# Attention decode backward on one core: long weight rows, gradients in place, scores of 32 rows, a zero fill issued alone

## The chip, the core and the metric

The kernel runs on one core of a Trainium2 chip. Times are device microseconds of that core. The kernel before takes 797.53 us, the median of two runs (797.41 and 797.66). The profile is one execution recorded by the hardware profiler, whose span, from the first to the last instruction, is 795.6 us.

## The reference

One decode step (two batches, one token, width 512) goes through a layer norm into two branches: attention over the last 4,096 of 32,768 cached positions, and a small MLP with squared ReLU. The output is `x + s * silu(u)`. All gradients are returned too.

```python
xn = layernorm(x)
q  = xn @ wq                                  # 32 heads of 128, 4 per K/V head
k, v = k_cache[:, :, -4096:], v_cache[:, :, -4096:]
p  = softmax(q @ k^T * 128**-0.5)
s  = (p @ v) @ wo
u  = relu(xn @ w1 + b1)**2 @ w2 + b2
out = x + s * silu(u)
# outputs: out, and d/d(x, k_cache, v_cache, wq, wo, w1, b1, w2, b2) for grad_out
```

The gradients of the two caches have the shape of the caches (2 x 8 x 32,768 x 128, 134 MB each). Outside the window of 4,096 positions they are zero, and the kernel has to write those zeros: 32 regions of 28,672 rows of 256 bytes, 234.88 MB.

## The kernel before

**Queues.** GpSimd (POOL) issues the zero fill, SyncE (SP) the loads of K, V, `w1`, `w2` and the last stores, ScalarE (ACT) the loads of `wq` and `wo` and the stores of gradients. All of them end on the same 16 DMA engines.

**Zero fill (lines 77 to 161).** The source is `zt`, 7,168 bytes of zeros per partition, which the DMA widens to bf16, so that one packet writes 14,336 bytes (56 rows of a cache). A fill covers 128 partitions x 4 such packets, a region. Every fourth region uses 32 rows a packet (8,192 bytes). `skip_plan` gives six regions a fill of 120 partitions in place of 128, which leaves one DMA engine out, after a tiny fill (`zf_tiny`) that is meant to set which. Nine fills are issued first (`ZF_FIRST`), the rest two or so per block between POOL's own work.

**Prologue (lines 205 to 311).** Norm, the MLP forward, and transposed copies of `w1` and `w2`.

**Blocks.** The loop over 8 K/V heads loads `wq` (two heads at once, 2,048-byte rows) and `wo` (4,096-byte rows) per head, transposes `wo`, computes q and the gradient `do` of the head's output for both batches, and has POOL build `bdq` and `bddo`: a row of q or do, repeated for 128 rows and masked by `maskbd`, 128 x 4,096, eight products of 128 x 1,024 per block (line 443). Then, for each batch (16 blocks in all): 32 transposes of K; scores as 32 products of 128 columns with a shifted window of `zq`, so that row `i * 32 + c` holds query i against chunk c; softmax over 128 x 128; 32 transposes of V; `o`; dp in the same form; `ds`; dq; and 8 + 8 outer products (lines 531 and 538) that make dv and dk in `dv_st` and `dk_st`, one buffer each. The gradient of `wo` for a head (`o_dependent_tail`, line 335) is made in the middle of a block and shares the `dv_st` buffer. The gradient of `wq` is stored for two heads at a time.

**Epilogue (lines 571 to 672).** The output, the MLP's backward with its two weight gradients, the gradient of x.

A scheduler orders the instructions of each engine from these dependences. The loads of block n + 1 wait until the buffers of block n - 1 (two per tensor) are free.

Of the kernel before, what the change touches and what calls it, by code (L numbers as in the profile page):

```python
# [8 lines left out]
ACT = mybir.ActivationFunctionType  # L9
# [8 lines left out]
def kernel(  # L18
# [28 lines left out]
    HQ = A_wq.shape[1] // DH  # L47
# [5 lines left out]
    DK = D // P  # L53
    SCALE = float(DH) ** -0.5
    EPS = 1e-5
    assert B == 2 and REP == 4 and NC_ == 32 and DH == P

    dma_zero = nc.gpsimd
    dma_load = nc.sync
    dma_store = nc.scalar  # L60

    const = ctx.enter_context(tc.tile_pool(name="const", bufs=1))
    attn = ExitStack()
    kvp = attn.enter_context(tc.tile_pool(name="kvp", bufs=2))
    kvt = attn.enter_context(tc.tile_pool(name="kvt", bufs=2))
    kt1 = attn.enter_context(tc.tile_pool(name="kt1", bufs=1))
    rowp = attn.enter_context(tc.tile_pool(name="rowp", bufs=1))
    wsl = attn.enter_context(tc.tile_pool(name="wsl", bufs=2))
    wsl1 = attn.enter_context(tc.tile_pool(name="wsl1", bufs=1))
    small = attn.enter_context(tc.tile_pool(name="small", bufs=3))  # L70
    hkp = attn.enter_context(tc.tile_pool(name="hkp", bufs=2))
# [4 lines left out]

    ZR = SK - W
    ZG = 56
    ZE = ZG * DH
    zt = const.tile([P, ZE], mybir.dt.uint8, name="zt")  # L80
    nc.vector.memset(zt[:].bitcast(F32), 0.0)

    zcur = [0]

    def _kof(n):
        for k in range(16, 0, -1):
            if n % k == 0:
                return k
        return 1

    def zf(o, q, r0, nent, rows_per_ent, zg=None):
        zg = zg or ZG
        b, hk = divmod(q, HKV)
        nr = nent * rows_per_ent
        if rows_per_ent % zg == 0:
            v = o[b, hk, r0:r0 + nr, :].rearrange("(r p g) d -> p r (g d)", p=nent, g=zg)
            src = zt[0:nent, 0:zg * DH].unsqueeze(1).to_broadcast([nent, rows_per_ent // zg, zg * DH])
        else:
            v = o[b, hk, r0:r0 + nr, :].rearrange("(p g) d -> p (g d)", p=nent)
            src = zt[0:nent, 0:rows_per_ent * DH]  # L100
        dma_zero.dma_start(out=v, in_=src)  # L101
        zcur[0] = (zcur[0] + _kof(nent)) % 16
        return r0 + nr

    SCRAP_Q = 2 * B * HKV - 1
    scrap_pos = [0]

    def zf_tiny(n):
        b, hk = divmod(SCRAP_Q % (B * HKV), HKV)
        p0 = scrap_pos[0]  # L110
        assert 0 < n and p0 + n <= DH
        dma_zero.dma_start(out=out_3[b, hk, ZR - 1:ZR, p0:p0 + n], in_=zt[0:1, 0:n])
        scrap_pos[0] = p0 + n
        zcur[0] = (zcur[0] + _kof(n)) % 16

    skip_plan = {3: (0, 4), 8: (4, 4), 13: (0, 4), 18: (4, 2), 23: (0, 4), 27: (3, 1)}
    ZG_OF = lambda qi: (ZG if qi % 4 != 3 else 32)
    zf_jobs = []

    def region_jobs(qi):  # L120
        o = out_2 if qi < B * HKV else out_3
        q = qi % (B * HKV)
        st = {"r": 0}

        zg = ZG_OF(qi)

        def j_skip():
            eng, nch = skip_plan[qi]
            adv = (eng + 1 - zcur[0]) % 16
            if adv:  # L130
                zf_tiny(adv)
            st["r"] = zf(o, q, st["r"], 120, nch * ZG)

        def j_main():
            rem = ZR - st["r"] - (P if qi == SCRAP_Q else 0)
            n_full = rem // (P * zg)
            if n_full:
                st["r"] = zf(o, q, st["r"], P, n_full * zg, zg)
            rem = ZR - st["r"] - (P if qi == SCRAP_Q else 0)
            if rem:  # L140
                nent = [n for n in (128, 64, 32, 16) if rem % n == 0][0]
                st["r"] = zf(o, q, st["r"], nent, rem // nent)
            if qi == SCRAP_Q:
                st["r"] = zf(o, q, st["r"], P - 1, 1)
                if scrap_pos[0] < DH:
                    zf_tiny(DH - scrap_pos[0])

        return ([j_skip] if qi in skip_plan else []) + [j_main]

    for qi in range(2 * B * HKV):  # L150
        zf_jobs.extend(region_jobs(qi))
    ZF_FIRST = 9

    def zf_issue(n):
        for _ in range(n):
            if zf_jobs:
                zf_jobs.pop(0)()

    zf_issue(ZF_FIRST)

# [3 lines left out]
    make_identity(nc, ident_f[:])  # L164
    eps_t = const.tile([P, 1], F32, name="eps_t")
    nc.vector.memset(eps_t[:], EPS)

# [16 lines left out]
    ds_rows = const.tile([B, D], BF16, name="ds_rows")  # L184

# [20 lines left out]

    with tc.tile_pool(name="pw", bufs=1) as pw:
# [6 lines left out]
        b2_bf = pw.tile([DK, P], BF16, name="b2_bf")  # L214
        dma_store.dma_start(out=b2_bf[:], in_=B_b2.rearrange("(k p) -> k p", p=P))
        w1 = pw.tile([P, DK, F], BF16, name="w1")
        dma_load.dma_start(out=w1[:], in_=B_w1.rearrange("(k p) f -> p k f", p=P))
        w2 = pw.tile([P, FK, D], BF16, name="w2")
        dma_load.dma_start(out=w2[:], in_=B_w2.rearrange("(p j) d -> p j d", j=FK))

        tp = ps_m.tile([P, DK, B], BF16, tag="m")
        for k in range(DK):
            nc.tensor.transpose(tp[:, k, :], x_bf[:, k * P:(k + 1) * P], ident_bf[0:B, 0:B])
        nc.vector.tensor_copy(out=xT_f[:], in_=tp[:])
        tp = ps_m.tile([P, DK, B], BF16, tag="m")
        for k in range(DK):
            nc.tensor.transpose(tp[:, k, :], go_bf[:, k * P:(k + 1) * P], ident_bf[0:B, 0:B])
# [4 lines left out]
        tp = ps_m.tile([P, DK], BF16, tag="m")  # L232
        nc.tensor.transpose(tp[:, :], b2_bf[:, :], ident_bf[0:DK, 0:DK])
        nc.vector.tensor_copy(out=b2T[:], in_=tp[:])
# [14 lines left out]
        tp = ps_m.tile([B, DK, P], BF16, tag="m")  # L249
        for k in range(DK):  # L250
            nc.tensor.transpose(tp[:, k, :], xnT[:, k, :], ident_bf[:, :])
        nc.vector.tensor_copy(out=xn_bf[:], in_=tp[:].rearrange("b k p -> b (k p)"))
# [12 lines left out]
        for dk in range(DK):  # L265
            for fk in range(FK):
                nc.tensor.matmul(ups[:, dk, :], lhsT=w2[:, fk, dk * P:(dk + 1) * P], rhs=h2T_bf[:, fk, :],
                                 start=(fk == 0), stop=(fk == FK - 1))
# [18 lines left out]
        tp = ps_m.tile([B, DK, P], BF16, tag="m")  # L287
        for k in range(DK):
            nc.tensor.transpose(tp[:, k, :], dsT_bf[:, k, :], ident_bf[:, :])
        nc.vector.tensor_copy(out=ds_rows[:], in_=tp[:].rearrange("b k p -> b (k p)"))  # L290
# [5 lines left out]
        for dk in range(DK):  # L296
            for fk in range(FK):
                jobs.append((w2[:, fk, dk * P:(dk + 1) * P], w2T, dk, fk * P))
# [14 lines left out]
    stage = attn.enter_context(tc.tile_pool(name="stage", bufs=1))  # L313
    bdp = attn.enter_context(tc.tile_pool(name="bdp", bufs=2))

    acc_s = const.tile([P, DK, B], F32, name="acc_s")
    nc.vector.memset(acc_s[:], 0.0)
    acc_dxn = const.tile([P, DK, B], F32, name="acc_dxn")
    nc.vector.memset(acc_dxn[:], 0.0)

    maskf = const.tile([P, NC_], F32, name="maskf")
    nc.vector.tensor_reduce(out=maskf[:], in_=ident_bf[:, :].rearrange("p (i c) -> p c i", i=REP), axis=AX.X, op=ALU.add)
    maskbd = const.tile([P, NC_, DH], BF16, name="maskbd")
    nc.vector.tensor_copy(out=maskbd[:], in_=maskf[:].unsqueeze(2).to_broadcast([P, NC_, DH]))
    NZ = 4
    zq_bufs, zdo_bufs = [], []
    for j in range(NZ):
        t = const.tile([P, 160], BF16, name=f"zq{j}")
        nc.vector.memset(t[:], 0.0)
        zq_bufs.append(t)  # L330
        t = const.tile([P, 160], BF16, name=f"zdo{j}")
        nc.vector.memset(t[:], 0.0)
        zdo_bufs.append(t)

    def o_dependent_tail(hk, oT_bf, wo_alt):
        tp = ps_m.tile([B, REP, P], BF16, tag="m")
        for i in range(REP):
            nc.tensor.transpose(tp[:, i, :], oT_bf[:, i, :], ident_bf[:, :])
        o_rows_alt = rowp.tile([B, REP, P], BF16, tag="o_rows_alt")
        nc.vector.tensor_copy(out=o_rows_alt[:], in_=tp[:].rearrange("b i d -> b (i d)").rearrange("b (p j) -> b j p", j=REP))  # L340
        tp = ps_m.tile([P, REP, B], BF16, tag="m")
        for j in range(REP):
            nc.tensor.transpose(tp[:, j, :], o_rows_alt[:, j, :], ident_bf[0:B, 0:B])
        oT_alt = hkp.tile([P, REP, B], BF16, tag="oT_alt")
        nc.vector.tensor_copy(out=oT_alt[:], in_=tp[:])
        sps = ps_m.tile([P, DK, B], F32, tag="m")
        for dk in range(DK):
            for j in range(REP):
                nc.tensor.matmul(sps[:, dk, :], lhsT=wo_alt[:, j, dk * P:(dk + 1) * P], rhs=oT_alt[:, j, :],
                                 start=(j == 0), stop=(j == REP - 1))  # L350
# [352 lines left out]
```

## Time and profile before

| what | value |
|---|---|
| median of the runs | 797.53 us |
| span of the profiled execution | 795.6 us |
| mean clock granted to TensorE | 0.691 |
| DMA, HBM read and written | 45.62 MB and 280.50 MB |
| mean us from issue to landing: K load, V load, dv store, dk store, zero fill of a region | 20.9, 16.6, 22.0, 17.1, 135.2 |
| POOL products (line 443) | 128, 267 us busy |

The profile cuts the span into 40 slices and gives the busy share of each engine and of the DMA in each. A queue's share is the time of its packets over the time of 16 engines. q0 is the zero fill, q1 what SP issues, q10 what ACT issues, q8 and q14 are instruction fetches. The waits name an idle engine, its line, and what ended its idle time.

### The profile page before, as it was taken

How to read it: one execution, taken by the hardware profiler on the slowest of the kernel's cores; microseconds unless marked ns; L12 is line 12 of the kernel's file. 1: busy time of each engine (PE TensorE's matmuls, PEld its weight loads, DVE VectorE, ACT ScalarE, POOL GpSimd, SP SyncE). 2: the span in 40 equal slices, each digit the busy share in tenths (PEclk: the TensorE clock that was granted, in tenths of full speed). 3: DMA queues.
4: the chain of work that ended last, by engine and by line, in shares of the span. 5: the costliest groups of instructions: out<-in, count | busy, mean ns of one | idle time of the engine just before them, and what ended most of it. 6: DMA issues, size and time to landing. Idle time of an engine off the chain costs nothing.

```text
span 795.6 us, 11174 instructions
## 1 busy us (share of the span) xinstructions
PE 402.2 (51%) x4776; PEld 277.0 (35%) x4776; DVE 265.6 (33%) x550; ACT 210.0 (26%) x384; POOL 315.3 (40%) x249
## 2 busy tenths in 40 slices
PE   4566444573446546634475358446733686276000
PEld 3466124352424444423272326243522353131000
DVE  3243322361323423611352136223611453754000
ACT  2232310360133314501342135203600450034000
POOL 3001791098109531881080719800826192700000
PEclk9978655895588659955697589656955795555555
DMA  9999999999999999999999999999999999999981
GB/s 361 421 422 424 427 427 423 431 416 417 423 428 424 417 420 428 421 421 421 428 420 422 424 426 423 425 422 430 422 420 422 430 425 420 431 429 425 416 340 57
DMA packets 37794, 326.85 MB, mean 411 GB/s; under 512 B 3008, under 2 KB 3144, under 8 KB 11016
## 3 DMA queue, kind: packets, MB, share of 16 engines
q0 software_dynamic: 20288, 234.89, 71.6%
q10 hardware_dynamic: 11296, 50.34, 16.5%
q1 hardware_dynamic: 6160, 40.91, 13.2%
q8 instruction: 37, 0.61, 0.3%
q14 instruction: 13, 0.11, 0.0%
HBM read 45.62 MB, written 280.50 MB: 410 GB/s over the span
## 4 chain that ended last, share of the span: by engine, by line
DMA 48%; PE 19%; DVE 9%; issue 6%; ACT 5%; POOL 2%; another core or an unknown queue 2%; ACTq 0%; POOLq 0%; DVEq 0%
DMA out_dram<-dv_st 20%; DMA knat<-in_A_k_cache_dram 15%; DMA out_dram<-dwo_st 7%; DMA out_dram<-zt 5%; ACT dv_st L193 3%; DMA out_dram<-dk_st 2%; PE ov L531 2%; PE s_ps L467 2%; PE ok L538 2%; PE tp L463 2%; PE dp_ps L506 2%; PE tp L495 1%; PE dq_ps L524 1%; DVE dk_st L195 1%
## 5 line engine op out<-in xcount | busy, mean ns | idle before, releaser
L443 POOL TENSOR_TENSOR bddo<-dorep,maskbd 128x1024 bf16<-128x1024 bf16 x64 | 133.6, 2114 | 90.5 <-ACT dorep L438 90.5
L443 POOL TENSOR_TENSOR bdq<-qrep,maskbd 128x1024 bf16<-128x1024 bf16 x64 | 133.4, 2110 | 0.0
L101 POOL DMA_DIRECT2D out_dram<-zt x42 | 32.2, 769 | 203.5 <-DMA out_dram<-zt 201.8
L463 PE MATMUL tp<-ident_bf,knat 128*128 128x128 bf16 x512 | 56.6, 280 | 74.8 <-DMA knat<-in_A_k_cache_dram 71.3
L463 PEld LDWEIGHTS <-knat 128*128 128x128 bf16 x512 | 44.7, 127 | 98.8 <-DMA knat<-in_A_k_cache_dram 72.8
L193 ACT CAST dv_st<-ov 128x512 bf16<-128x512 f32 x80 | 44.4, 593 | 125.3 <-PE ov L531 81.2
L531 PE MATMUL ov<-bddo,p_blk 128*128 128x512 bf16 x128 | 51.4, 486 | 50.3 <-ACT dv_st L193 39.6
L195 DVE CAST dv_st<-ov 128x512 bf16<-128x512 f32 x48 | 33.2, 693 | 100.7 <-PE ov L531 57.9
L355 PE MATMUL wps<-ds_rows,o_rows_alt 2*128 2x512 bf16 x32 | 17.4, 600 | 73.0 <-ACT dwo_st L193 73.0
L538 PE MATMUL ok<-bdq,ds_blk 128*128 128x512 bf16 x128 | 46.2, 422 | 15.9 <-DVE dk_st L195 6.0
L195 DVE COPY kT<-tp 128x1024 bf16<-128x1024 bf16 x48 | 32.8, 682 | 58.4 <-PE tp L463 58.4
L193 ACT CAST dk_st<-ok 128x512 bf16<-128x512 f32 x80 | 44.6, 589 | 26.7 <-PE ok L538 22.5
L495 PE MATMUL tp<-ident_bf,vnat 128*128 128x128 bf16 x512 | 42.9, 235 | 7.6 <-DVE vT L195 4.5
L495 PEld LDWEIGHTS <-vnat 128*128 128x128 bf16 x512 | 36.6, 107 | 26.3 <-issue 24.4
L195 DVE CAST dk_st<-ok 128x512 bf16<-128x512 f32 x48 | 32.8, 689 | 28.1 <-PE ok L538 24.8
L195 DVE CAST dwo_st<-wps 128x512 bf16<-128x512 f32 x16 | 11.1, 691 | 85.5 <-DMA out_dram<-dv_st 81.8
L193 ACT CAST dwo_st<-wps 128x512 bf16<-128x512 f32 x16 | 8.7, 588 | 112.0 <-DMA out_dram<-dv_st 111.6
L195 DVE COPY vT<-tp 128x1024 bf16<-128x1024 bf16 x48 | 32.3, 682 | 14.7 <-PE tp L495 14.5
L531 PEld LDWEIGHTS <-p_blk 128*128 128x128 bf16 x128 | 12.7, 119 | 59.6 <-ACT dv_st L193 25.5
L538 PEld LDWEIGHTS <-ds_blk 128*128 128x128 bf16 x128 | 10.3, 103 | 40.2 <-DVE dv_st L195 17.3
L519 PEld LDWEIGHTS <-ds_blk 128*128 128x128 bf16 x16 | 1.7, 104 | 64.2 <-issue 64.2
L195 DVE COPY woT_s<-tp 128x1024 bf16<-128x1024 bf16 x8 | 19.5, 2432 | 10.5 <-PE tp L394 10.5
(240 smaller groups left out, 674.9 us busy)
## 6 DMA issues: line engine op xcount, KB each, us to landing
out_dram<-zt POOLq DMA_DIRECT2D x25, 7168.0 KB, 135.2
out_dram<-zt POOLq DMA_DIRECT2D x4, 6720.0 KB, 146.6
vnat<-in_A_v_cache_dram SPq DMA_DIRECT2D x16, 1024.0 KB, 16.6
knat<-in_A_k_cache_dram SPq DMA_DIRECT2D x16, 1024.0 KB, 20.9
out_dram<-dv_st ACTq DMA_DIRECT2D x16, 1024.0 KB, 22.0
out_dram<-dk_st ACTq DMA_DIRECT2D x16, 1024.0 KB, 17.1
out_dram<-zt POOLq DMA_DIRECT2D x1, 6144.0 KB, 100.5
out_dram<-zt POOLq DMA_DIRECT2D x1, 5120.0 KB, 98.6
```

The costliest lines, as they stand in the source:

```text
L101: dma_zero.dma_start(out=v, in_=src)
L193: nc.scalar.copy(out=out_ap, in_=in_ap)
L195: nc.vector.tensor_copy(out=out_ap, in_=in_ap)
L355: nc.tensor.matmul(wps[:], lhsT=o_rows_alt[:, j, :], rhs=ds_rows[:, :], start=True, stop=True)
L443: nc.gpsimd.tensor_tensor(out=bd[:, c0:c0 + BDC, :], in0=rep[:, :].unsqueeze(1).to_broadcast([P, BDC, DH]), in1=maskbd[:, c0:c0 + BDC, :], ...
L463: nc.tensor.transpose(tp[:, j, :], knat[:, g * 8 + j, :], ident_bf[:, :])
L467: nc.tensor.matmul(s_ps[:], lhsT=zq[:, 31 - c:159 - c], rhs=kT[:, c, :], start=(c == 0), stop=(c == NC_ - 1))
L495: nc.tensor.transpose(tp[:, j, :], vnat[:, g * 8 + j, :], ident_bf[:, :])
L506: nc.tensor.matmul(dp_ps[:], lhsT=zdo[:, 31 - c:159 - c], rhs=vT[:, c, :], start=(c == 0), stop=(c == NC_ - 1))
L524: nc.tensor.matmul(dq_ps[:], lhsT=knat[:, c, :], rhs=dsT[:, c, :], start=(c == 0), stop=(c == NC_ - 1))
L531: nc.tensor.matmul(ov[:], lhsT=p_blk[:, :], rhs=bddo[:, g * 4:(g + 1) * 4, :].rearrange("p c d -> p (c d)"), start=True, stop=True)
L538: nc.tensor.matmul(ok[:], lhsT=ds_blk[:, :], rhs=bdq[:, g * 4:(g + 1) * 4, :].rearrange("p c d -> p (c d)"), start=True, stop=True)
```

## The change

Work is moved between queues and stages; what is computed stays.

- **Weights.** `wq` and `wo` are loaded whole on SP in the prologue and stay in memory. Partition p holds four adjacent rows of `wq` (32 KB) and 32 adjacent rows of `wo` (32 KB); `w1` is laid out in the same way (14 KB), as `w2` was. q and do of all heads are computed in the prologue.
- **Gradients in place.** The gradient of `wq` is written over `wq` head by head and stored once after the loop. The gradient of `wo` is written over `wo` at the end of the epilogue and stored once. The gradients of `w1` and `w2` are made after that of x.
- **Scores.** 32 rows of 512: 8 products of 512 columns in place of 32 of 128. The softmax joins 8 groups of rows with `group_sum`, a masked 32 x 32 transpose and reduction.
- **Block diagonals.** 32 x 1,024 in place of 128 x 4,096, made by DVE from PSUM. The outer products have 32 rows to contract in place of 128.
- **Zero fill.** All 42 fills are issued one after the other, all of 128 partitions but the last pieces; no `skip_plan`. POOL does nothing else after the identities.
- **Buffers.** `stage` has 2 buffers of dv and of dk, which nothing else uses; K's load stands before V's.

```diff
-    skip_plan = {3: (0, 4), 8: (4, 4), 13: (0, 4), 18: (4, 2), 23: (0, 4), 27: (3, 1)}
-    ZG_OF = lambda qi: (ZG if qi % 4 != 3 else 32)
...
+    for qi in range(ZQ):
+        o, q = (out_2, qi) if qi < B * HKV else (out_3, qi - B * HKV)
+        if qi < ZQ - 1:
+            zf(o, q, 0, P, ZG, ZR // (P * ZG))
+        else:
+            r = zf(o, q, 0, P, ZG, 3)
+            r = zf(o, q, r, P, 30)
+            r = zf(o, q, r, 64, 1)
+            for rows in (8, 9, 10, 11, 12, 13, 14, 19):
+                r = zf(o, q, r, 34, rows)
...
-        dma_load.dma_start(out=w1[:], in_=B_w1.rearrange("(k p) f -> p k f", p=P))
+        dma_load.dma_start(out=w1[:], in_=B_w1.rearrange("(p k) f -> p k f", k=DK))
...
+        dma_load.dma_start(out=wo[:], in_=A_wo.rearrange("(p j) m -> p j m", j=NJ))
+        dma_load.dma_start(out=wq[:], in_=A_wq.rearrange("(p k) n -> p k n", k=DK))
...
-    stage = attn.enter_context(tc.tile_pool(name="stage", bufs=1))
+    stage = attn.enter_context(tc.tile_pool(name="stage", bufs=2))
...
-            for (bd, rep) in ((bddo, dorep), (bdq, qrep)):
-                for c0 in range(0, NC_, BDC):
-                    nc.gpsimd.tensor_tensor(out=bd[:, c0:c0 + BDC, :],
-                                            in0=rep[:, :].unsqueeze(1).to_broadcast([P, BDC, DH]),
-                                            in1=maskbd[:, c0:c0 + BDC, :], op=ALU.mult)
...
+    def group_sum(out_t, src, op, mask, comb, negate=False):
+        tmp = small.tile([R, R], F32, tag="gs")
+        nc.vector.tensor_scalar(out=tmp[:], in0=mask[:].rearrange("p g i -> p (g i)"), scalar1=src[:, 0:1],
+                                scalar2=None, op0=comb)
+        nc.vector.tensor_reduce(out=out_t[:], in_=tmp[:], axis=AX.X, op=op, apply_transpose=True, negate=negate)
...
+        rp = ps_m.tile([R, P], F32, tag="m")
+        nc.tensor.matmul(rp[:], lhsT=zr[:].rearrange("p g i -> p (g i)"), rhs=ident_bf[:, :], start=True, stop=True)
+        bd = bdp.tile([R, G, DH], BF16, tag="bd" + tag)
+        nc.vector.tensor_tensor(out=bd[:], in0=rp[:].unsqueeze(1).to_broadcast([R, G, DH]),
+                                in1=m8[:].unsqueeze(2).to_broadcast([R, G, DH]), op=ALU.mult)
...
+    def scores(out_ps, nat, zbuf):
+        for gp in range(G // 2):
+            tp = ps_t.tile([P, 8, P], BF16, tag="pt")
+            for j in range(8):
+                nc.tensor.transpose(tp[:, j, :], nat[:, gp * 8 + j, :], ident_bf[:, :])
+            tT = kvt.tile([P, 8, P], BF16, tag="tT")
+            evac(tT[:], tp[:], eng=("act" if gp == 3 else "dve"))
+            for gg in range(2):
+                g = gp * 2 + gg
+                nc.tensor.matmul(out_ps[:], lhsT=zbuf[:, ZO - REP * g:ZO - REP * g + R],
+                                 rhs=tT[:, gg * CC:(gg + 1) * CC, :].rearrange("p c s -> p (c s)"),
+                                 start=(g == 0), stop=(g == G - 1))
...
+        for cc in range(CC):
+            for gh in range(2):
+                ov = ps_o.tile([P, 4, DH], F32, tag="o")
+                nc.tensor.matmul(ov[:], lhsT=src[:, cc * P:(cc + 1) * P], rhs=bd[:, gh * 4:(gh + 1) * 4, :],
+                                 start=True, stop=True)
+                evac(st[:, gh * 4:(gh + 1) * 4, cc, :], ov[:], eng=("act" if n in (0, 1, 3, 4, 6) else "dve"))
...
-        if hk % 2 == 1:
-            dma_store.dma_start(out=out_4[:, (hk - 1) * REP * DH:(hk + 1) * REP * DH].rearrange("(k p) n -> p k n", p=P), in_=dwq_st[:])
+                evac(wq[:, k, hk * REP * DH:(hk + 1) * REP * DH], wps[:])
...
+    dma_store.dma_start(out=out_4.rearrange("(p k) n -> p k n", k=DK), in_=wq[:])
...
+    for j in range(NJ):
+        wps = ps_o.tile([P, D], F32, tag="o")
+        nc.tensor.matmul(wps[:], lhsT=o_rows[:, j:N:NJ], rhs=ds_rows[:, :], start=True, stop=True)
+        evac(wo[:, j, :], wps[:])
+    dma_store.dma_start(out=out_5.rearrange("(p j) m -> p j m", j=NJ), in_=wo[:])
```

## The prediction, written before the result was known

> **What bounds the kernel now.** I read the slices of the page first, then its queues, then windows at the end of the span, then the chain and the waits.
>
> ```profile
> DMA  9999999999999999999999999999999999999981
> GB/s 361 421 422 424 427 427 423 431 416 417 423 428 424 417 420 428 421 421 421 428 420 422 424 426 423 425 422 430 422 420 422 430 425 420 431 429 425 416 340 57
> DMA packets 37794, 326.85 MB, mean 411 GB/s; under 512 B 3008, under 2 KB 3144, under 8 KB 11016
> ...
> q0 software_dynamic: 20288, 234.89, 71.6%
> q10 hardware_dynamic: 11296, 50.34, 16.5%
> q1 hardware_dynamic: 6160, 40.91, 13.2%
> ```
>
> From the second slice to the 38th the 16 DMA engines are never free and move 416 to 431 GB/s. No compute engine is near that: PE is busy 402.2 of 795.6 us, DVE 265.6, POOL 315.3. So the span is bytes, plus what the head and the tail leave unused. Zero fill (q0) is 72% of the bytes and the change keeps all of them.
>
> ```profile
> 700.00:740.00 40.00, 25.56 (x79) 9.68 (x75) 16.69 (x33) 15.51 (x27) 0.51 (x1) 0.54 1.04 426
> 740.00:760.00 20.00, 0.00 (x0) 0.00 (x0) 0.00 (x0) 0.00 (x0) 0.00 (x0) 0.50 1.03 410
> 760.00:770.00 10.00, 0.00 (x0) 0.00 (x0) 0.00 (x0) 0.00 (x0) 0.00 (x0) 0.50 0.89 354
> 770.00:780.00 10.00, 0.00 (x0) 0.00 (x0) 0.00 (x0) 0.00 (x0) 0.00 (x0) 0.50 0.58 228
> 780.00:790.00 10.00, 0.00 (x0) 0.00 (x0) 0.00 (x0) 0.00 (x0) 0.00 (x0) 0.50 0.11 41
> 790.00:796.00 6.00, 0.00 (x0) 0.00 (x0) 0.00 (x0) 0.00 (x0) 0.00 (x0) 0.50 0.04 14
> ```
>
> These are stages of the span: length, busy time of PE, PE load, DVE, ACT, POOL, clock, DMA share, GB/s. All computing is over before 740 us. The rate then falls in steps: 354, 228, 41. A full rate is about 430, so 41 is one or two engines out of 16. The DMA engines do not finish together, and the last runs alone for some 11 us.
>
> ```profile
> POOL out_dram L101 <- DMA out_dram<-zt: 201.8, 16, 31.2
> ACT dwo_st L193 <- DMA out_dram<-dv_st: 111.6, 8, 23.5
> POOL bddo L443 <- ACT dorep L438: 90.5, 10, 20.0
> ```
>
> The waits show that the compute side has slack to lose: it waits for landings (the page's chain is 48% DMA), and the shared `dv_st` buffer costs ACT 111.6 us. All this lies beside a full DMA.
>
> **The price of a packet.** The trace keeps start, duration, queue and size of each packet. I fitted the time of 16 busy engines in windows of 4 us, from 20 to 740 us, by packet counts. One engine is held by a zero packet of 14,336 B for 531.5 ns, by one of 8,192 B for 304.9, by a K/V load of 8,192 B for 306.3, by a store of 8,192 B for 322.7, by a `wo`/`dwo` row of 4,096 B for 171.3, and by a `wq`/`dwq` row of 2,048 B for 93.9. The lone last engine confirms the scale: 8,192 B packets every 303.5 ns, 27.0 GB/s, so 432 for 16. A PE instruction fetch (q8, 37 packets of 16,384 B) takes about 950 ns and the packet behind it is late by 0.13 to 0.4 us: 1.33 us at most.
>
> Test on before, in engine-us: zero fill 13,288 x 0.5315 + 4,992 x 0.3049 + 134 for odd rows = 8,719; loads 4,096 x 0.3063 = 1,255; stores 4,096 x 0.3227 = 1,322; `wo` rows 2,048 x 0.1713 = 351; `wq` rows 4,096 x 0.0939 = 385; `w1`, `w2` and gradients 279; fetches 49. Sum 12,360, over 16 engines 772.5, from the first packets at 4.1 us: a mean end at 776.6. The last zero packets per engine in the records give 16 ends: 756.1, 765.6 (two), 766.7, 773.8, six in 776.6 to 780.6, four in 783.3 to 783.9, and 795.5. Their mean is 776.6. So 795.5 = 776.6 of mean work + 18.9 of uneven work.
>
> **The change, part by part.**
>
> Weights in long rows: `wq`, `wo`, `w1`, `w2` and gradients are 24.12 MB, at 0.03707 ns per byte (the 14,336 B row; nothing in this trace is longer) 894 engine-us, against 351 + 385 + 279 = 1,015: minus 121, or 7.6 us of span. Rows of 32 KB could cost as much per byte as the 8 KB stores (0.0394): then minus 4.1 us. I take 7.6, as the 14,336 B weight rows fit the same line.
>
> Zero fill in 14,336 B rows alone: 16,384 x 0.5315 = 8,708, minus 11, 0.7 us. Fewer PE instructions: 9,505 in the built program before, 7,538 after; at 64 B each (37 x 16,384 B over 9,505) 29 fetches, minus 10, 0.7 us. Loads and stores of K and V stay: 1,255 + 1,322. New sum 12,218, over 16 is 763.6, from 4.1 us: mean end 767.7, 8.9 earlier.
>
> Even work: the plan before sent six fills of 120 rows, each leaving one engine out (32 packets = 17 us in the four large ones). The records show what they do. Around 100 us, behind the first, one engine is at its next packets at 83.7 and the 15 others between 100.1 and 102.2. So without skips the engines are even to 2 us after an eighth of the run. The 15 form two groups about 1.2 us apart, 8 and 7, and five q8 fetches and one of q14 had been made by then: the fetches seem to go round the engines. The wide spread (three leading engines, one lagging by 15) appears behind the later skips. After the change every fill but the last pieces is 128 rows, 8 per engine. I take a skew of 1.5 us (bounds 0.7 and 19, the skew of before).
>
> A rule speaks against this: the Trainium skill (DMA: Bandwidth & Descriptors, section Latency and other measured facts) says that DMA engines 7 and 15 are usually slower than the others under software descriptors, with no figure. Two slow engines would need lighter loads, and an even fill would end with them. The row at 100 us shows 15 engines within 2 us with no slow pair, so the sum follows the row; by the rule a lag of 2 us per 100 would be 16 us at the end, 790.
>
> Last pieces: 835 KB in eight fills of 34 rows. POOL keeps eight fills in flight, so the last two go out only when the 30-row and 1-row fills have landed on all engines: about 2 us for landing, 1 to 2 for two issues (0.77 each in the page) and the data. How 34 rows are spread is not in this trace; the same page (Why a DMA increments its semaphore by 16) has k as the largest divisor up to 16, so 2 engines of 17 rows, 3.1 us for 19-row packets (17 x 4,864 B), or, for some copies, 3 rows per engine, 0.5 us. The 127-row fill here went 8 to 15 engines and 7 to one, which is the second kind. I take a tail of 6 us behind even ends (bounds 3 and 9), of which the mean already holds 1.9.
>
> Sum: 767.7 - 1.9 + 1.5 + 6 = 773.3 us of span. The median stands 1.9 above the span of this profile (797.53 against 795.6): **775 us**, minus 2.8%.
>
> What lies beside it, at nothing, if computing ends before the fill. POOL loses 128 products of 2.1 us (267 us) and its waits no longer hold anything up; the fills are all it issues. DVE takes two 32 x 1024 products a block, bounded by 1.4 us (1,024 elements at 0.69 per 512) and 2.4 (the slow `woT_s` copy of 1,024); I take 1.5; `pm` and the two 512-wide products cost 0.29 to 0.7 each. DVE per block: 6 x 0.68 + 6 x 0.69 + 2 x 1.5 + 3 x 0.7 + about 3 of small ones = 16 us. ACT: 2 x 1.01 + 10 x 0.59 + 2 = 10. PE: transposes 3.5 + 2.7, scores 4.8 (same columns as before at 76 ns per 128), contractions 4, outer products 6.1, the projection part 2: 23. With `stage` doubled, dwo out of the loop, I expect 25 to 32 us a block, where before took about 41. Moved queues: `wo` and `wq` (8.4 MB) now stand on SP before K/V; four weight loads are 12 MB, at about 60% of the rate 47 us. The first K/V load also waits for the prologue's memory (PE, DVE, ACT): nothing but zero fill is late behind it. I start attention at 100 us, end it by 100 + 16 x 30 = 580, and give 60 us to the gradients, now 62 outer products at the end: 640 us. The cover is 125 us. It is gone when a block takes over 38 us ((768 - 100 - 60) / 16); each further us of block then costs 16.
>
> **The rivals.**
>
> Uneven ends remain (as before, some cause other than skips). For: the lag of 15 us isn't traced to one skip. Against: the 100 us row. Price: 767.7 + 19 + 2 = 789 us, minus 1%.
>
> Fetches sit on one engine (the one that ends slower). Place: the queue of zero fill on that engine, with no skip to relieve it. 29 x 1.33 = 39 us behind the others, 767.7 x about 1 + 37 + 2 = 806 us, plus 1.1%. It decides from about 22 fetches on the same engine (29 us). For: six skips stood in the plan for some load. Against: by 98 us five fetches would have put one engine 6 us back; none was over 2.
>
> Computing becomes the bound: blocks of 42 us or more, end beyond 835 us. For: PE's clock falls to 0.5 to 0.7, and before took 41. Against: much of that 41 was landings and `dv_st`.
>
> The long rows don't move faster: mean end 775, with even ends 783 us.
>
> **How the numbers follow.** Forecast 0.72 (768 to 782); uneven or no gain from rows 0.18 (782 to 792); one engine with fetches 0.05 (800 to 810); computing 0.05 (800 to 850). The range 767 to 790 leaves out a bit under 2 in 10. A measurement tells 2% from no change, the line is at 781.6 us: faster 0.74, within 0.20, slower 0.06.
>
> **What would show it.** Right: mean rate near 423 to 425 GB/s over the span, computing over by 600 to 680 us, then slices of zero fill alone at 430, packets under 8 KB down from 11,016 to about 3,000, and a rate that falls from 430 to nothing in under 10 us. Wrong: a tail of 30 GB/s for tens of us (one engine), or DMA slices below 9 in the middle (computing bounds). More than 1.05 of the per-byte price in the weights' slices would put the long-row step wrong.

## The result, and the profile after

The changed kernel took 784.94 us (median of 2 runs, 784.84 to 785.05), the kernel before 797.53: a ratio of 0.984, 95% interval 0.981 to 0.987. It is faster by 1.6%, where 2.8% was forecast. That is above the line at 781.6 us and outside the 768 to 782 that was given 0.72; it lies in the 782 to 792 that was given 0.18, for uneven ends or no gain from rows. The profiled execution has a span of 783.0 us, 1.9 under the median.

Three words used below: a *fetch* is a packet of TensorE's instructions (q8); the *lag* of an engine is how far its end lies behind the mean end of the 16 DMA engines, unless the median is named; an *engine-us* is one DMA engine busy for 1 us.

First the slices and the queues of the changed kernel's page. Columns of a queue: packets, MB, share of 16 engines.

```profile
DMA  9999999999999999999999999999999999999992
GB/s 356 431 429 431 430 428 424 423 427 425 425 427 426 424 424 426 424 426 425 426 426 424 425 424 425 424 427 424 427 426 435 421 432 428 431 434 434 432 430 107
DMA packets 28362, 326.70 MB, mean 417 GB/s; under 512 B 2441, under 2 KB 2450, under 8 KB 2850
...
q0 software_dynamic: 17504, 234.88, 72.3%
q1 hardware_dynamic: 5626, 49.29, 15.9%
q10 hardware_dynamic: 5192, 41.95, 13.3%
q8 instruction: 29, 0.48, 0.2%
```

The DMA engines are full in 39 slices of 40, and rates are higher and steadier than before: 421 to 435 GB/s from the second slice to the 39th, with packets under 8 KB down from 11,016 to 2,850. The steps of the bytes are right in kind. q8 fell from 37 instruction fetches to 29, as computed. The mean over the span, 417, is under the 423 that was named as the sign of success, and the fall to nothing takes some 20 us (below), not under 10.

Then the stages. Columns: stretch, length, busy us and count of PE, PE load, DVE, ACT, POOL, clock, DMA share, GB/s.

```profile
500.00:600.00 100.00, 86.99 (x578) 38.72 (x577) 46.06 (x92) 32.97 (x57) 3.72 (x5) 0.57 1.04 428
600.00:700.00 100.00, 44.54 (x253) 20.49 (x250) 37.61 (x61) 18.17 (x31) 2.44 (x4) 0.54 1.04 428
700.00:740.00 40.00, 0.00 (x0) 0.00 (x0) 0.00 (x0) 0.00 (x0) 1.01 (x2) 0.50 1.04 433
740.00:760.00 20.00, 0.00 (x0) 0.00 (x0) 0.00 (x0) 0.00 (x0) 0.51 (x1) 0.50 1.04 432
760.00:770.00 10.00, 0.00 (x0) 0.00 (x0) 0.00 (x0) 0.00 (x0) 0.51 (x1) 0.50 0.75 290
770.00:780.00 10.00, 0.00 (x0) 0.00 (x0) 0.00 (x0) 0.00 (x0) 1.51 (x3) 0.50 0.12 44
780.00:784.00 4.00, 0.00 (x0) 0.00 (x0) 0.00 (x0) 0.00 (x0) 0.00 (x0) 0.50 0.16 54
```

Computing is over at 661 us, and its last store has landed by 682; the zero fill then runs alone at 432 until 760. After that the rate breaks, and from 770 to 780 it is 44 GB/s: one engine out of 16, with a few small rows beside it. The same stretch in 40 slices of 1.1 us:

```profile
DMA  9999999999999999999999875431000000306000
GB/s 456 443 417 430 430 417 417 430 443 430 430 430 430 443 469 430 417 443 402 419 409 355 321 283 198 161 111 53 39 26 26 26 21 28 114 26 245 22 0 0
```

Fifteen engines are through by about 769 us; then come slices of 26 GB/s, the rate that the prediction had found for one lone engine (27). The last 34-row pieces wait for it: they are the 114 and the 245 at the end. To see all 16 engines I took from the packet records the time at which each one reaches the one-row fill, which stands just before the pieces in all of its queues (times from the span's start; the prediction counted the records from 2.2 us earlier, in all its figures alike, so its 767.7 is 765.5 here):

```
changed kernel  762.4 762.6 762.8 763.2 763.4 764.5 766.6 766.8 766.8
                766.9 767.8 767.8 768.3 768.7 768.8 777.9    mean 766.6
```

The fifteen stand within 6.4 us. The sixteenth is 11.3 behind the mean, and the span ends 5.1 us after it. At the ends of earlier fills the last engine was behind the median by 1.0 us when this stood at 49 us, 3.0 at 120, 6.5 at 278 and 9.6 at 328, by when 14 of the 29 fetches had been made. From there to 631 us it moved between 9.2 and 13.2, with no clear growth over the other 15, and was 21.4 once, at 652, beside the stores of the last gradients. In the four fills that ended from 684 to 735, with no computing left, it was 11.1 each time. So it grew only beside computing, though not evenly with it; a cleaner series comes with the products put back, below.

### The profile page after: what moved, and what is told of

The parts are those of the page before. It is cut to its first block, busy times and chain, and to the rows that moved or that the text cites. A ratio compares the mean times of both kernels' runs of the same rounds, so it can differ in the third digit from the quotient of the medians.

```text
span 783.0 us, 8997 instructions
## 1 busy us (share of the span) xinstructions
PE 526.7 (67%) x3794; PEld 251.4 (32%) x3794; DVE 318.6 (41%) x683; ACT 212.6 (27%) x349; POOL 30.3 (4%) x50
## 3 DMA queue, kind: packets, MB, share of 16 engines
q0 software_dynamic: 17504, 234.88, 72.3%
## 4 chain that ended last, share of the span: by engine, by line
another core or an unknown queue 89%; DMA 6%; POOL 3%; issue 1%; DVE 0%; POOLq 0%
DMA out_dram<-zt 6%; POOL out_dram L91 3%; DVE zt L79 0%; POOLq L629 0%
## 5 line engine op out<-in xcount | busy, mean ns | idle before, releaser
L137 ACT CAST st<-ov 128x512 bf16<-128x512 f32 x160 | 89.5, 588 | 170.9 <-PE ov L390 170.5
L139 DVE CAST st<-ov 128x512 bf16<-128x512 f32 x96 | 66.3, 690 | 93.3 <-PE ov L390 92.3
L139 DVE COPY tT<-tp 128x1024 bf16<-128x1024 bf16 x96 | 65.0, 679 | 46.0 <-PE tp L359 45.7
L359 PE MATMUL tp<-ident_bf,vnat 128*128 128x128 bf16 x512 | 64.8, 290 | 1.2 <-DMA vnat<-in_A_v_cache_dram 1.2
L390 PE MATMUL ov<-bd,ds_bf 32*128 32x512 bf16 x128 | 59.5, 530 | 5.9 <-DVE st L139 3.1
L390 PE MATMUL ov<-bd,p_bf 32*128 32x512 bf16 x128 | 58.5, 541 | 5.6 <-DVE bd L351 5.1
L137 ACT COPY tT<-tp 128x1024 bf16<-128x1024 bf16 x32 | 32.3, 1010 | 93.6 <-PE tp L359 93.6
L351 DVE TENSOR_TENSOR bd<-rp,m_151 32x1024 bf16<-32x1024 f32 x32 | 38.6, 1208 | 15.3 <-PE rp L349 15.3
L364 PE MATMUL s_ps<-tT,zq_171 128*32 128x512 bf16 x32 | 17.8, 608 | 6.1 <-ACT tT L137 4.4
L380 PE MATMUL ps<-t,knat 128*128 128x4 bf16 x512 | 18.7, 167 | 0.0
L364 PE MATMUL s_ps<-tT,zq_167 128*32 128x512 bf16 x32 | 16.2, 595 | 3.1 <-DVE tT L139 3.1
## 6 DMA issues: line engine op xcount, KB each, us to landing
knat<-in_A_k_cache_dram SPq DMA_DIRECT2D x16, 1024.0 KB, 16.8
```

Source lines behind the costliest of these rows:

```text
L137: nc.scalar.copy(out=out_ap, in_=in_ap)
L139: nc.vector.tensor_copy(out=out_ap, in_=in_ap)
L351: nc.vector.tensor_tensor(out=bd[:], in0=rp[:].unsqueeze(1).to_broadcast([R, G, DH]), in1=m8[:].unsqueeze(2).to_broadcast([R, G, DH]), op= ...
L359: nc.tensor.transpose(tp[:, j, :], nat[:, gp * 8 + j, :], ident_bf[:, :])
L364: nc.tensor.matmul(out_ps[:], lhsT=zbuf[:, ZO - REP * g:ZO - REP * g + R], rhs=tT[:, gg * CC:(gg + 1) * CC, :].rearrange("p c s -> p (c s) ...
L380: nc.tensor.matmul(ps[:], lhsT=nat[:, c, :], rhs=tT[:, cc, g * REP:(g + 1) * REP], start=(c == 0), stop=(c == NC_ - 1))
```

## The experiments

Two theories stood at first. **Fetches**: TensorE's instruction fetches fall more often on one DMA engine than on the others, and each costs it about 1.3 us. **Slow engine**: one engine is slower at all of its rows, or has more loads and stores, whatever TensorE does. Against both stands what else the change brought: how much of the gain is the long rows, and how much the even fills.

### More fetches

```diff
+    for _ in range(700):
+        nc.tensor.matmul(pd[:, :], lhsT=ident_bf[:, :], rhs=ident_bf[:, 0:B], start=True, stop=True)
```

The products stand at the end of the program; nothing reads them but a copy. They ran from 640 to 690 us, beside the last gradients and their stores, and not only beside the fill alone.

> 700 products into a scratch tile are added at the end of PE's program, so 1,400 more instructions, 5 more fetches of 16,384 B, in the stretch (from about 690 us) where only zero fill runs and where the last DMA engine's lag stands still at 9 us in the changed kernel. If the lag is the work of instruction fetches that all land on one DMA engine: 5 x 1.3 us more, the last engine ends 6 to 7 us later and the time is about 791 us. If fetches go round the engines: the mean end moves by 0.4 us, the lag stays at 11 us and the time is 785 to 786 us.

Measured: 788.49 us, ratio to before 0.989 (0.987 to 0.990); q8 has 35 packets. The mean of the 16 engines rose by 0.5 us, the last one by 3.5 (from 777.9 to 781.4), the last but one by 1.1. That lies between what one engine for all fetches (8 us) and an even round (0.5 us) would give: 0.5 us of lag over the mean for each further fetch. At 1.3 us each (the 8 engine-us over six), the 3.5 us of the last engine would be two or three of the six: some of the fetches hit that engine, not all.

### Leave one engine out

```diff
+        dma_load.dma_start(out=out_2[0, 0, 0:F15, :].rearrange("(r p g) d -> p r (g d)", p=15, g=28),
+                           in_=zt[0:15, :].bitcast(BF16).unsqueeze(1).to_broadcast([15, 32, 28 * DH]))
```

> 13,440 rows of the first region are filled from SP by one DMA of 15 partitions (32 packets of 7,168 B each) instead of by 128; the bytes are the same. If such a DMA takes the 15 lowest engines and the lagging engine is the 16th, that engine has 8.5 us less to do and the others 0.6 us more: the ends come together, time about 776 us. If the lagging engine is one of the 15: one engine ends 8 us before the rest, the lag stays, time 785 to 786 us.

Measured: 805.96 us, ratio 1.011 (1.009 to 1.012). The stretches show why it misses:

```profile
20.00:40.00 20.00, 7.34 (x71) 6.93 (x71) 3.31 (x15) 1.58 (x2) 0.74 (x1) 1.00 1.03 432
40.00:60.00 20.00, 13.94 (x154) 9.60 (x154) 8.12 (x19) 6.07 (x6) 0.74 (x1) 0.91 1.01 309
60.00:80.00 20.00, 11.84 (x86) 7.39 (x84) 7.03 (x6) 10.39 (x8) 0.00 (x0) 0.75 1.04 293
80.00:100.00 20.00, 16.24 (x164) 9.25 (x164) 6.96 (x19) 9.91 (x17) 0.74 (x1) 0.91 1.02 376
```

While the fill of 15 partitions runs, all engines are busy (share 1.01 to 1.04) at 293 to 309 GB/s in place of 430: one of its rows of 7,168 B took 730 ns in the median, where rows of that size took 289 in the fills of the later experiments. The mean end went to 780.7. One engine was indeed left out and ended first, at 754.9. The last, at 798.8, is 8.2 behind the next: the lagging engine is one of the 15 that were loaded. So the run spares the wrong engine, and tells that the lagging one is not the one that 15 rows leave out.

### Short rows again

```diff
-        dma_load.dma_start(out=wq[:], in_=A_wq.rearrange("(p k) n -> p k n", k=DK))
+        for n0 in range(0, N, 1024):
+            dma_load.dma_start(out=wq[:, :, n0:n0 + 1024], in_=A_wq.rearrange("(p k) n -> p k n", k=DK)[:, :, n0:n0 + 1024])
```

The same for `wo` in rows of 4,096 B, and for both gradients.

> wq and its gradient move in rows of 2,048 B and wo and its gradient in rows of 4,096 B again, on the same queues as in the changed kernel. If a short row costs what the profile of before says (93.9 and 171.3 ns against 0.037 ns per byte), 7 us more on every engine: time about 792 us. If the long rows gave nothing: 785 us. The lag of the last engine stays in both.

Measured: 788.20 us, ratio 0.988 (0.987 to 0.990). That is 3.3 us over the changed kernel; the mean end moved from 766.6 to 771.5, by 4.9, and the last engine by 3.2 (from 777.9 to 781.1). The long rows are a real gain, smaller than the prediction's 7.6 us (7.1 of them for these four tensors) and near its lower bound of 4.1.

### The kernel before, without its skips

```diff
-    skip_plan = {3: (0, 4), 8: (4, 4), 13: (0, 4), 18: (4, 2), 23: (0, 4), 27: (3, 1)}
+    skip_plan = {}
```

> The kernel before with an empty skip plan: all 32 regions filled by 128 partitions, nothing else changed. If the skips hit the wrong engines: the mean end stays at 774 us of the span, the engines come within 4 us of each other except for one that lags by 11 to 13 us as in the changed kernel, time 788 to 791 us. If the skips did relieve engines that needed it: the lag grows to 30 us or more, time above 803 us.

Measured: 791.76 us, ratio 0.993 (0.991 to 0.994): 5.7 us faster than before, and just over the 788 to 791 expected. Its last stretches, in the same columns:

```profile
770.00:780.00 10.00, 0.00 (x0) 0.00 (x0) 0.00 (x0) 0.00 (x0) 0.00 (x0) 0.50 0.44 170
780.00:791.00 11.00, 0.00 (x0) 0.00 (x0) 0.00 (x0) 0.00 (x0) 0.00 (x0) 0.50 0.05 19
```

The skips had given the time away, as the prediction said: the three engines that led are gone (15 engines now reach their last one-row fill at 769.7 to 776.9). But one engine still ends alone, at 788.1, 13.6 behind the mean, with 37 fetches. So the long rows and the other parts of the change did not bring the lone engine: the kernel before has it too, once its skips are gone.

### A plain tail

```diff
-            r = zf(o, q, 0, P, ZG, 3)
-            r = zf(o, q, r, P, 30)
-            r = zf(o, q, r, 64, 1)
-            for rows in (8, 9, 10, 11, 12, 13, 14, 19):
-                r = zf(o, q, r, 34, rows)
+            zf(o, q, 0, P, ZG, ZR // (P * ZG))
```

> The changed kernel with its last region filled by whole-width rows like the others, without the 34-row pieces at the end. If the end is one DMA engine that lags, the pieces save nothing: the last fill is over where that engine is (about 778 us by the changed kernel's trace, 779 with its final rows), the span is 781 to 783 us and the time 783 to 785. If the pieces do even out the ends, taking them away costs several us: the time is 788 us or more.

Measured: 783.15 us (782.82 to 783.27), ratio 0.982 (0.980 to 0.983), 1.8 us faster than with the pieces. They level nothing: each puts its 34 rows on 12 engines, three on most of them, and the last ones go out only when the lagging engine has landed earlier ones.

### Name the engine

```diff
+                dma_store.dma_start(out=out_2[0, qi, r:r + n, :].rearrange("(r p g) d -> p r (g d)", p=kk, g=28),
+                                    in_=zt[0:8 * kk:8, :].bitcast(BF16).unsqueeze(1).to_broadcast([kk, 56, 28 * DH]))
```

Three such fills, with `kk` 12, 8 and 4. The source rows are eight partitions apart, and the slow stretch of the fill from 15 adjacent ones doesn't come back (414 to 427 GB/s in slices 2 to 10). The spacing isn't shown as the reason: these fills also have fewer rows and are issued by ACT in place of SP.

> The changed kernel with three further fills at the start, whose rows go to engines by partition, so that four groups of four engines get about 0, 16, 32 and 48 us more of zero rows. The lagging engine is then seen some 9 to 12 us behind one of the groups, which tells the four among which it is. If the lag belongs to one fixed engine, it is again one engine, 9 to 12 us behind its own group. If the lag is made by chance of the queues, no single engine stands so far behind its group, or it is the most loaded group that spreads. The time is no measure here: the most loaded engines end about 24 us over the mean, so 790 to 812 us.

Measured: 800.23 us in one execution, a span of 797.9, and these ends, which I split into fours by the steps of 16 us:

```
no extra   740.7 744.4 744.6 745.9
one fill   756.6 761.7 761.9 762.1
two fills  775.2 776.2 781.8 786.4
three      788.2 788.3 790.9 793.0
```

The first two groups have nobody 9 us behind; the third has one, 10 us behind its first two. So the lagging engine is most likely the one that serves the fifth, sixth, seventh or eighth row of a fill. The reading is not firm, since the third group has a second straggler, 6 us behind.

### The same traffic without attention

```diff
-        knat, vnat = kvs.pop(blk)
...
+        kvs.pop(blk)
+        dma_store.dma_start(out=out_3[b, hk, kwin, :].rearrange("(p c) d -> p c d", c=NC_), in_=st0[:])
+        dma_store.dma_start(out=out_2[b, hk, kwin, :].rearrange("(p c) d -> p c d", c=NC_), in_=st0[:])
```

> The changed kernel with its block loop reduced to the loads of K and V and to stores of as many rows: it leaves out the attention, its gradients and wq's gradient, so that TensorE has about 1,600 instructions in place of 7,500, and every row that moves to and from HBM for K, V, dK and dV stays. If TensorE's instruction fetches make one engine lag, about 6 or 7 fetches are left and the last engine ends 2 to 3 us over the mean: a span of 768 to 774 us. If the lag comes of the loads and stores themselves, or of an engine that is slower at all of its rows, it stays 9 to 12 us over the mean and the span at 778 to 783 us.

The attention, its gradients and the gradient of `wq` are left out. Measured: 772.39 us in one execution, span 770.3. TensorE's row and the fetches' row of its page:

```profile
PE 108.3 (14%) x850; PEld 62.4 (8%) x850; DVE 70.4 (9%) x134; ACT 52.2 (7%) x69; POOL 30.3 (4%) x50
...
q0 software_dynamic: 17504, 234.88, 73.5%
q1 hardware_dynamic: 5626, 49.29, 16.1%
q10 hardware_dynamic: 5192, 41.95, 13.0%
q8 instruction: 6, 0.10, 0.0%
```

q0, q1 and q10 carry the same packets as in the changed kernel, to the packet; q8 has 6 in place of 29. All 16 engines end between 761.4 and 765.2, mean 762.5: the lag over the mean is 2.7 us in place of 11.3. With this traffic and six fetches no engine is slow by itself.

```profile
740.00:760.00 20.00, 0.00 (x0) 0.00 (x0) 0.00 (x0) 0.00 (x0) 0.51 (x1) 0.50 1.04 432
760.00:770.00 10.00, 0.00 (x0) 0.00 (x0) 0.00 (x0) 0.00 (x0) 1.51 (x3) 0.50 0.52 182
```

### The products back

```diff
+        for _ in range(184):
+            nc.tensor.matmul(pd[:, :], lhsT=ident_bf[:, :], rhs=ident_bf[:, 0:B], start=True, stop=True)
```

In each block, in the kernel without attention.

> The kernel without the attention (its gradients and wq's gradient are left out as well), with 184 products of 128 by 2 in each block that nothing of the output reads, so that TensorE has 7,588 instructions again and fetches them while the same loads and stores go on. If fetching TensorE's instructions makes the lag, it is back: 28 or 29 fetches, one engine 8 to 12 us over the mean and a span of 776 to 781 us. If something else that the attention does makes it (its waits, VectorE and ScalarE), the last engine stays 2 to 4 us over the mean and the span at 769 to 773 us.

Measured: 782.24 us in one execution, span 779.8, 29 fetches. The lone engine is back:

```profile
q8 instruction: 29, 0.48, 0.2%
...
740.00:760.00 20.00, 0.00 (x0) 0.00 (x0) 0.00 (x0) 0.00 (x0) 0.51 (x1) 0.50 1.04 430
760.00:770.00 10.00, 0.00 (x0) 0.00 (x0) 0.00 (x0) 0.00 (x0) 0.51 (x1) 0.50 0.61 231
770.00:780.00 10.00, 0.00 (x0) 0.00 (x0) 0.00 (x0) 0.00 (x0) 1.51 (x3) 0.50 0.16 56
```

```
without attention  761.4 to 765.2, all 16                    mean 762.5
products back      761.3 to 762.1 (7), 765.1 to 767.4 (8), 774.8    mean 764.9
```

DVE (72.9 us busy against 70.4) and ACT (52.3 against 52.2) do the same work in both. 23 fetches more raise the mean by 2.4 us (38 engine-us, 1.7 for each fetch) and set one engine 10 us behind it. Set side by side in the order of their ends, seven engines hardly move, eight lose 3 to 4 us each, and the last loses 9.6 of the 38. As the records don't name the engines, the lone one may have stood further forward without the products; then it lost up to 13.4. So a quarter to a third of the cost fell on one engine.

The fetches of this kernel come early, 27 of 29 by 273 us, while the loads and stores of K and V go on to about 420. Its fills therefore show the lag with and without fetches in the same traffic:

```
products back: a fill's end, us   110   137   172   208   244   280   316   422   546
fetches so far                      4     8    12    18    23    27    27    27    29
lag over the mean, us             2.0   5.8   7.4   9.0  10.2  10.7  10.9  10.9   9.8
```

Without the products, at four fetches, the lag stayed at 3.0 to 3.6 us in all fills from 110 to 393 us. So it grows while fetches are made and stands still when they stop, but less for each later fetch.

### Spare that engine

```diff
+    LEAN, REPL = 4, 40
...
+        n = LEAN * REPL * (ZG // 2)
+        dma_store.dma_start(out=out_2[0, 0, 0:n, :].rearrange("(r p g) d -> p r (g d)", p=LEAN, g=ZG // 2),
+                            in_=zt[0:8 * LEAN:8, :].bitcast(BF16).unsqueeze(1).to_broadcast([LEAN, REPL, ZG // 2 * DH]))
```

Both with the plain tail; the first with `LEAN, REPL = 7, 32`.

> The kernel with the plain tail, in which 6,272 rows of the first zero region are filled from seven partitions by ACT, so that seven engines get about 9.1 us more of rows (32 rows of 7,168 B at 0.286 us) and the other nine, by equal shares of what that takes off, 4.0 us less. If the lagging engine is the eighth, as the fills in steps leave open (they showed it among the fifth to the eighth), it is one of the nine: the last engine ends 4 us earlier and the time is 779 us (778 to 781). If it is the fifth, sixth or seventh, it gets the 9.1 us as well and the time is 788 us.

> The same with 4,480 rows from four partitions, about 11.4 us more on the first four engines and 2.8 us less on the other twelve. If the lagging engine is any of the fifth to the eighth, the last engine ends 2.8 us earlier and the time is 780.3 us (779 to 782). If the steps were misread and it is one of the first four, it gets the 11.4 us as well and the time is 791 us; if lag is made anew wherever the load is lightest, the time stays at 783.

Measured: seven rows 787.63 us, ratio 0.988 (0.986 to 0.989); four rows 780.57 us (780.42 to 780.62), ratio 0.979 (0.977 to 0.980), the fastest of all complete kernels here. Both are within 0.4 us of one of the times that their expectations named: four rows spare the engine, seven load it as well. So it serves the fifth, sixth or seventh row. The end of the four-row version:

```profile
740.00:760.00 20.00, 0.00 (x0) 0.00 (x0) 0.00 (x0) 0.00 (x0) 0.00 (x0) 0.50 1.04 432
760.00:770.00 10.00, 0.00 (x0) 0.00 (x0) 0.00 (x0) 0.00 (x0) 0.00 (x0) 0.50 0.70 290
770.00:779.00 9.00, 0.00 (x0) 0.00 (x0) 0.00 (x0) 0.00 (x0) 0.00 (x0) 0.50 0.17 70
```

and of the plain tail without it:

```profile
760.00:770.00 10.00, 0.00 (x0) 0.00 (x0) 0.00 (x0) 0.00 (x0) 0.00 (x0) 0.50 0.78 321
770.00:782.00 12.00, 0.00 (x0) 0.00 (x0) 0.00 (x0) 0.00 (x0) 0.00 (x0) 0.50 0.05 22
```

After 770 us the plain tail moves 22 GB/s for 12 us, less than one engine's full rate; the other moves 70 for 9 us. The bytes of the lone engine's last microseconds have gone to engines that had ended earlier.

## Why the prediction was right in direction and its gain too large

**What held.** The bound: DMA is full until the fill ends and computing hides behind it. The skips as a loss (5.7 us when they alone go). Fewer fetches, 29. Long rows as a gain. Computing off the path. And the time lies in the range of 767 to 790, within 1.3% of the number, but in the part of it that was given the smaller chance.

**The step that failed** is "I take a skew of 1.5 us". The measured lag of the last engine over the mean is 11.3 us: 9.8 us more, while the number missed by 9.9. That the other two errors, 3.0 us up and 2.8 down (below), cancel is luck. The prediction read the kernel before at 100 us, saw 15 engines within 2 us, and took that as even for the whole run. By then five of 37 fetches had been made. A quarter to a third of five fetches at 1.33 us is 1.7 to 2.2 us, no more than the row showed; it could not tell "even" from "a third on one engine". The text had worked out what 2 us in 100 would come to (16 at the end, 790) and left it aside. The rule of the Trainium skill that it weighed there (DMA: Bandwidth & Descriptors, section Latency and other measured facts: two engines slower under software descriptors) was nearer to the size, yet not by its mechanism: with the same 17,504 packets of the software queue and 6 fetches no engine stands alone, and with 29 one does, not two.

**The rival "uneven ends remain"**, from some cause other than the skips, is what came about. Its price, 789 us, took over the skew of before, 19 us; the lag in the changed kernel was 11.3.

**The rival "fetches sit on one engine"** named the mechanism and priced it in one form alone, all 29 on one engine, 806 us. "By 98 us five fetches would have put one engine 6 us back; none was over 2" excludes that form and not the one that happened. The lags measured go with the count of fetches:

```
               no attention   products back   short rows   changed   more fetches   before, no skips
fetches              6             29             29          29          35              37
PE busy, us        108            196            521         527         547             405
lag, us            2.7            9.9            9.6        11.3        14.3            13.6
```

At the end of a run that is 0.3 to 0.5 us for each fetch, over kernels that otherwise differ in much. The time for which TensorE works doesn't order them: 196 and 521 us with 29 fetches give the same lag. The share is no fixed price, since within a run the first fetches added more than the last.

**Terms that were mis-sized.** The mean end before the last pieces: 763.6 forecast (767.7 less 2.2 of the records' start and 1.9 of pieces), 766.6 measured. Most of these 3.0 us are the long rows. `wq`, `wo` and their gradients were to bring 7.1 of the 7.6 (351 + 385 - 622 engine-us over 16, the last from 16.8 MB at 0.03707); undone, they cost 4.9. I fitted the time of 16 busy engines by packet counts again, each packet shared out over the windows of 4 us that it spans: 88 and 165 ns for the short rows of that experiment, where the prediction had 93.9 and 171.3, and 1,221 ns for a row of 32 KB in the changed kernel (0.0373 ns a byte). That is (362 + 337 - 625) / 16 = 4.6 us. So it is mainly the short rows that were priced too high. The tail: 6 us forecast for the pieces behind even ends, 3.2 measured from the lagging engine's last row to the last data (777.9 to 781.1). With these in place the sum is 775.0 + 3.0 + 9.8 - 2.8 = 785.0, against 784.94 measured.

**Computing** was put at nothing, rightly. It ended at 661 us, in the 600 to 680 named, though later than the 640 of the sum; the 16 blocks ran from 119 us (first transpose) to 585 (last outer product), so a block took 29 us, in the 25 to 32 named. TensorE's part of a block was too low. Groups of the changed kernel (out<-in, count | busy us, mean ns | idle before):

```profile
L359 PE MATMUL tp<-ident_bf,knat 128*128 128x128 bf16 x512 | 58.0, 276 | 30.2 <-DMA knat<-in_A_k_cache_dram 15.9
L359 PE MATMUL tp<-ident_bf,vnat 128*128 128x128 bf16 x512 | 64.8, 290 | 1.2 <-DMA vnat<-in_A_v_cache_dram 1.2
L390 PE MATMUL ov<-bd,ds_bf 32*128 32x512 bf16 x128 | 59.5, 530 | 5.9 <-DVE st L139 3.1
L390 PE MATMUL ov<-bd,p_bf 32*128 32x512 bf16 x128 | 58.5, 541 | 5.6 <-DVE bd L351 5.1
```

Over 16 blocks these are 7.7 us of transposes a block (6.2 forecast) and 7.4 of outer products (6.1). The scores (line 364, 119.2 us in all) took 7.5, where 4.8 was forecast for the same columns. PE is busy for 87 to 92 of each 100 us from 200 to 600, at a granted clock of 0.57 to 0.65, so a block holds about 26 us of it (29 x 0.89), not 23. The cover, from the end of computing to the mean end of the engines, was about 105 us in place of 125, and hid it all.

**Where the 12.6 us came from**, parts undone one at a time: skips 5.7 (in the kernel before), long rows 3.3 (in the changed one). The rest, 3.6, wasn't run by itself; as an estimate, eight fetches fewer at 0.6 us each (788.49 - 784.94 over six) would be 4.7, and the pieces take back 1.8.

## What to carry to other kernels

When all DMA engines are full, the time is that of the last engine and not the mean: look at the close-up of the last 20 us, and divide its rate by one engine's. A small spread early in a run should be multiplied out to its end before it is called even, and a rival should be priced in its weak form as well as in the strong one. TensorE's instruction count costs DMA time even where TensorE is off the critical path; rows that go by number to engines can be used to give the one that pays for it less to do.

## What the runs showed of the hardware

- TensorE's instructions are fetched through the same DMA engines: one packet of 16,384 B for about 260 of its instructions (29 for 7,588 counted in the changed kernel's groups of PE and PE load). Each took some 1.3 us (six more fetches, 8 engine-us) to 1.7 us (23 more, 38 engine-us) of one engine, and not evenly: a quarter to a third of the cost fell on one engine. Why so much of it does stayed open; the records do not name the engine.
- A fill read from 15 adjacent partitions moved 293 to 309 GB/s with all engines busy; fills of 4 to 12 rows read from partitions eight apart showed no such stretch (414 to 427 GB/s beside those of 4, 8 and 12 rows). They were issued from another queue too, so the cause is not shown.
- A fill of few rows loads few engines: 15 rows left one engine 14 us ahead of the rest (754.9 against 769.0), and fills of 12, 8 and 4 rows set the ends in steps. That the rows go to the engines in one fixed order is inferred from the fills of 7 and 4 rows, which ended within 0.4 us of what that order gives (787.63 and 780.57 us).
